# Local attention scores: two heads per matmul, with block-diagonal queries

## The chip, the cores and the metric

The kernel runs on one core of one Trainium2 chip. The metric is the device time of one execution in microseconds (us); lower is better.

Engine names as the profile has them: PE is TensorE, DVE is VectorE, ACT is ScalarE, POOL is GpSimd.

## The reference

Two attention branches over one input x of 2048 positions and width 1024 (32 heads of 32), mixed by a gate. Branch A is linear attention. Branch B, which the change touches, lets each position attend to 8 positions: itself and every second one before it.

```python
def _B_ref(x, wqkv, wo):            # cut: shapes, head transposes
    W, dil = 8, 2
    off = jnp.arange(W) * dil
    idx = pos[:, None] - off[None, :]
    mask = idx >= 0
    ...
    logits = jnp.einsum("bhsd,bhswd->bhsw", q, kg) * scale
    logits = jnp.where(mask[None, None, :, :], logits, -1e9)
    attn = _softmax(logits, axis=-1)
    o = jnp.einsum("bhsw,bhswd->bhsd", attn, vg)
    return ... @ wo

g = _sigmoid((x * gate_w).sum(-1, keepdims=True))
return g * _A_ref(x, A_wqkv, A_wo) + (1 - g) * _B_ref(x, B_wqkv, B_wo)
```

## The kernel before

The kernel loads x with even and odd positions apart, so that the step of 2 becomes a step of 1. A window of 57 queries then needs 64 keys. A *block pair* (in the code a "fill") is two such windows, h = 0 and 1; there are 18 of them. Each has a block of scores, an exponential, a mask, and later a block of values with the sums of the weights:

```python
def fill(e_, qs, nq, offs):                 # nq is 57, or 56 in the last of each half
    ...                                     # loads of the values
    def s_fn(e):
        for c in range(8):                  # 8 groups of 4 heads; head 4c+j on rows 32j
            for h in range(2):
                for j in range(4):
                    last = e.matmul(SO[j].ap(c * nq, (c + 1) * nq)[64 * h:64 * h + 64, :],
                        kT[32 * j:32 * j + 32, c, <64 keys>], qT[32 * j:32 * j + 32, c, <nq queries>],
                        start=True, stop=True, tile_position=(32 * j, 64 * h))
        return last
    P.op("pe", s_fn, 0.55, mode="r", ..., name="S")          # 64 matmuls of 57 columns
    ...                                     # ACT: exp of the scores; DVE: times the mask
    after(PVLAG, values)                    # three slots later: 64 value matmuls and 8 of sums
```

`P.op` only records an operation. A list scheduler written in Python then fixes, before anything runs, the order of the instructions on each engine, by priorities (the order of recording, mostly) and by a table of estimated durations. `slot` is called after each group of 8 dense matmuls, so "two slots later" means about two such groups later:

```python
def slot(rate):
    slot_n[0] += 1
    while later and later[0][0] <= slot_n[0]:
        later.pop(0)[1]()
    ...                                     # starts the next fill when its turn has come
```

Between the fills run dense groups: projections, and the keys of branch A, whose state is summed by blocks of 32 small matmuls ("kv"). When the last state block is done, these operations follow:

```python
# DVE: kva -> kvb, its transpose kvT, then sixteen small copies, which lay out zsel
for c in range(4):
    for r in range(4):
        P.op("dve", lambda e, ...: e.tensor_copy(zsel[32 * r:..., c:8:4, k:k + 1], kva[32 * c:..., r:8:4, 32:33]), 0.1, ...)

def fold(I, jh):                            # state times output weights; called four times
    four = [main.next() for _ in range(4)]  # four of the eight PSUM banks
    ...                                     # 16 matmuls of 32x32 tiles, 512 columns
    for c in range(4):
        move(ws[1][:, 4 * I + c, ...], four[c].ap, 512, four[c], ...)   # four copies out, ACT or DVE

for n, (u, j) in enumerate(nums):           # the queries of branch A, one dense group each
    numer(u, j)                             # one bank; ACT: exp; DVE: two operations
    ...
    if n in (2, 4, 6, 8):
        fold((n - 2) // 4, (n - 2) // 2 % 2)
```

## Time and profile before

| | old kernel |
|---|---|
| time, median | 492.45 us (three runs, 492.34 to 493.23) |
| span of the profiled run | 490.9 us |
| PE busy | 485.7 us, 99% |
| DVE busy | 274.5 us, 56% |
| ACT busy | 166.9 us, 34% |
| score matmuls | 18 blocks of 64 |

From the profile's page of the old kernel: busy time of each engine with its share of the span and its instructions, then the chain that ended last, by engine.

```profile
PE 485.7 (99%) x5123; PEld 226.5 (46%) x5123; DVE 274.5 (56%) x487; ACT 166.9 (34%) x287; POOL 5.1 (1%) x27
...
PE 95%; SPq 2%; DVE 2%; DMA 1%; issue 0%
```

PE bounds the kernel, so a saving counts only if it shortens PE's row, and a delay only if PE waits for it.

The chain in order of time, old kernel, around two score blocks (start in us, duration in us, engine and line; line 1326 are dense matmuls, 1418 scores, 1437 values, 1444 sums):

```profile
126.56 0.63 PE ps_all L1418 x64
127.20 5.29 PE ps_all L1326 x24
132.48 0.21 PE ps_all L1437 x24
132.69 0.19 PE ps_all L1444 x8
132.88 0.32 PE ps_all L1437 x40
...
138.49 0.63 PE ps_all L1418 x63
```

The row of PE is an unbroken alternation of dense groups and small blocks. (One matmul record of 64 is missing in the last line; some records are, so I count weight loads where a count matters.)

The groups of the small matmuls, old kernel (line, engine, operation, shapes, count, then busy us and mean ns of one):

```profile
L1418 PE MATMUL ps_all<-qT,kT 32*64 32x57 bf16 x1024 | 11.2, 200 | 0.0
L1444 PE MATMUL ps_all<-E,ones 64*32 64x456 bf16 x128 | 6.1, 351 | 0.0
```

A mean of 200 ns per matmul says nothing of the cost, because many overlap: in the records used below, the eight matmuls of a round, one on each array tile, start within 0.023 us. What a block costs has to be read from starts.

The table of stretches, old kernel (window in us, its length, then busy time of PE, PEld, DVE, ACT, POOL):

```profile
126.00:319.00 193.00, 193.00 (x3700) 96.13 (x3699) 118.11 (x200) 100.39 (x150) 0.00 (x0) 1.00 0.19 56
319.00:337.00 18.00, 17.94 (x144) 7.15 (x142) 16.34 (x46) 10.11 (x27) 0.00 (x0) 1.00 0.01 2
```

The scores lie where DVE is busy 61% of the time. The second is the stage of the folds that follows.

The old kernel's chain shows the same stage from 319.01 us on, until the second fold:

```profile
319.01 0.44 DVE kva L1527
...
325.79 0.61 DVE pq L1339
...
326.44 0.44 PE ps_all L1571 x16
```

These 7.4 us are nearly all of the chain's 2% for DVE.

### The profile page before, as it was taken

To read this page: it belongs to the slowest core of one execution; us is meant where nothing else is said; L and a number is where in the kernel's file an instruction comes from. 1 tells how busy PE (TensorE), PEld (TensorE's weight loads), DVE (VectorE), ACT (ScalarE), POOL (GpSimd) and SP (SyncE) were. 2 spreads that over 40 slices of the span, in tenths; PEclk is the share of its full clock that TensorE was granted. 3 is DMA by queue.
4 is the path that set the end of the run, shared out by engine and by line. 5 is a ranking of instruction groups with operands and counts; after the bars stand their busy time and mean duration, and the time that the engine had idled before them with its cause. 6 is when DMAs were issued, how large, how long until landed. Compare 5 with 4: busy or idle time off the path is not lost.

```text
span 490.9 us, 11427 instructions
## 1 busy us (share of the span) xinstructions
PE 485.7 (99%) x5123; PEld 226.5 (46%) x5123; DVE 274.5 (56%) x487; ACT 166.9 (34%) x287; POOL 5.1 (1%) x27
## 2 busy tenths in 40 slices
PE   8999999999999999999999999999999999999997
PEld 3444444444444444555454454444444444444443
DVE  2121336899677777465555645596865735334434
ACT  2111121212443344665655556355423323010000
POOL 3000000000000000000000000000000000000000
PEclk9999999999999999999999999999999999999999
DMA  8999993222003045211000100501673406101212
GB/s 208 216 197 271 356 366 100 86 87 85 13 24 109 24 127 146 65 28 43 24 24 24 36 12 4 171 3 22 172 193 80 115 13 180 44 23 45 85 68 89
DMA packets 51069, 48.82 MB, mean 99 GB/s; under 512 B 20161, under 2 KB 38977, under 8 KB 51010
## 3 DMA queue, kind: packets, MB, share of 16 engines
q1 hardware_dynamic: 50322, 47.40, 34.9%
q8 instruction: 42, 0.69, 0.6%
q10 hardware_dynamic: 688, 0.59, 0.4%
q14 instruction: 17, 0.14, 0.1%
HBM read 34.34 MB, written 9.44 MB: 89 GB/s over the span
## 4 chain that ended last, share of the span: by engine, by line
PE 95%; SPq 2%; DVE 2%; DMA 1%; issue 0%
PE ps_all L1326 77%; PE ps_all L1647 11%; PE ps_all L1418 2%; PE ps_all L1437 2%; SPq L1300 1%; PE ps_all L1519 1%; DMA w<-in_B_wqkv_dram 1%; PE ps_all L1444 1%; DVE zsel L1561 1%; SPq L1305 1%; PE ps_all L1598 0%; DVE pq L1339 0%; PE ps_all L1571 0%; DVE e L1337 0%; DVE w L1357 0%
## 5 line engine op out<-in xcount | busy, mean ns | idle before, releaser
L1326 PE MATMUL ps_all<-w,xT 128*128 128x512 bf16 x960 | 213.8, 379 | 0.7 <-DMA xT<-in_A_x_dram 0.6
L1326 PE MATMUL ps_all<-xT,w 128*128 128x512 bf16 x768 | 170.7, 379 | 0.0
L1326 PEld LDWEIGHTS ps_all<-w,xT 128*128 128x128 bf16 x960 | 91.1, 98 | 109.8 <-DMA xT<-in_A_x_dram 2.0
L1326 PEld LDWEIGHTS ps_all<-xT,w 128*128 128x128 bf16 x768 | 73.8, 98 | 89.0 <-issue 1.8
L1647 PE MATMUL ps_all<-w,qT 128*128 128x512 bf16 (+1 forms) x264 | 55.6, 373 | 0.0
L1647 PEld LDWEIGHTS ps_all<-w,qT 128*128 128x128 bf16 x264 | 25.8, 98 | 29.7
L1337 DVE TENSOR_SCALAR e<-e 128x512 bf16<-128x512 bf16 x64 | 18.3, 290 | 34.3 <-ACT e L1335 17.1
L1357 DVE CAST vst<-ps_all 128x512 bf16<-128x512 f32 x15 | 10.4, 691 | 44.3 <-PE ps_all L1326 44.3
L1424 ACT ACTIVATE E<-ps_all 128x1824 bf16<-128x1824 f32 (+1 forms) x18 | 30.4, 1687 | 10.1 <-PE ps_all L1418 9.4
L1335 ACT ACTIVATE e<-ps_all 128x512 bf16<-128x512 f32 x32 | 19.1, 597 | 42.8 <-PE ps_all L1326 42.8
L1427 DVE TENSOR_TENSOR E<-E,msk 128x1824 bf16<-128x1824 bf16 (+1 forms) x18 | 19.8, 1102 | 22.4 <-ACT E L1424 22.4
L1651 DVE SCALAR_TENSOR_TENSOR o<-ps_all,gm,xT 128x512 bf16<-128x512 f32 (+1 forms) x25 | 18.0, 728 | 23.2 <-PE ps_all L1647 22.2
L1333 ACT ACTIVATE e<-ps_all 128x512 bf16<-128x512 f32 x32 | 19.1, 597 | 26.6 <-PE ps_all L1326 25.8
L1358 ACT ACTIVATE vst<-ps_all 128x512 bf16<-128x512 f32 x17 | 10.1, 597 | 49.7 <-PE ps_all L1326 45.5
L1287 DVE TENSOR_TENSOR mx<-mx,kT 128x1024 bf16<-128x1024 bf16 x32 | 20.8, 688 | 9.3 <-ACT kT L1358 9.2
L1287 DVE TENSOR_TENSOR mx<-mx,qT 128x1024 bf16<-128x1024 bf16 x32 | 20.8, 686 | 6.9 <-ACT qT L1361 6.7
L1456 DVE TENSOR_TENSOR qT<-ps_all,L 128x456 bf16<-128x456 f32 (+1 forms) x36 | 21.0, 627 | 6.2 <-ACT L L1454 5.0
L1339 DVE SCALAR_TENSOR_TENSOR pk<-ps_all,e 128x512 bf16<-128x512 f32 x32 | 21.9, 688 | 0.7
L1453 ACT ACTIVATE L<-ps_all 128x456 f32<-128x456 f32 (+1 forms) x36 | 17.8, 547 | 12.4 <-PE ps_all L1437 12.4
L1358 ACT ACTIVATE kT<-ps_all 128x512 bf16<-128x512 f32 x16 | 9.6, 597 | 34.5 <-PE ps_all L1326 34.5
L1361 ACT ACTIVATE qT<-ps_all 128x512 bf16<-128x512 f32 x16 | 9.6, 597 | 31.5 <-PE ps_all L1326 31.5
L1614 DVE TENSOR_TENSOR xT<-xT,rb 128x512 bf16<-128x512 bf16 x24 | 16.2, 688 | 6.6 <-DMA rb<-rc_hbm 6.4
(72 smaller groups left out, 285.6 us busy)
## 6 DMA issues: line engine op xcount, KB each, us to landing
rb<-rc_hbm SPq DMA_DIRECT2D x32, 256.0 KB, 4.8
w<-in_A_wqkv_dram SPq DMA_DIRECT2D x6, 1024.0 KB, 9.3
v<-vB_hbm SPq DMA_DIRECT2D x36, 128.0 KB, 2.8
vB_hbm<-vst SPq DMA_DIRECT2D x32, 128.0 KB, 5.9
w<-in_B_wqkv_dram SPq DMA_DIRECT2D x4, 1024.0 KB, 9.5
xn<-in_A_x_dram SPq DMA_DIRECT2D x16, 256.0 KB, 2.8
out_dram<-o SPq DMA_DIRECT2D x15, 256.0 KB, 2.0
w<-in_A_wo_dram SPq DMA_DIRECT2D x8, 256.0 KB, 3.9
```

The source lines that it names most:

```text
L1287: P.op("dve", lambda e, m=m, op=op: e.tensor_tensor(m[:, 0:n], m[:, 0:n], src, op), 0.08 + n / 1920.0, reads=[m.all(), reg], writes=[m.all()],
L1326: last = e.matmul(bank.ap(), lhs(dc), rhs(dc), start=(dc == 0), stop=(dc == 7))
L1333: P.op("act", lambda e: e.activation(e_[:, :], bank.ap(), ACT.Exp), act(512), reads=[bank.iv], writes=[e_.all()])
L1335: P.op("act", lambda e: e.activation(e_[:, :], bank.ap(), ACT.Exp, accum_out=qe[:, col:col + 1]), act(512) + 0.1, reads=[bank.iv], writes= ...
L1337: P.op("dve", lambda e: e.tensor_scalar(e_[:, :], e_[:, :], 1.0, 1e-6, op0=ALU.min, op1=ALU.add), 0.25, reads=[e_.all()], writes=[e_.all()])
L1339: P.op("dve", lambda e: e.scalar_tensor_tensor(out=dst, in0=bank.ap(), scalar=0.0, in1=e_[:, :], op0=ALU.max, op1=ALU.add), dps(512), read ...
L1358: fa = lambda e: e.activation(dst, src(), ACT.Copy)
L1424: P.op("act", lambda e: e.activation(E[:, 0:32 * nq].rearrange("p (j q) -> p j q", j=4), ps[:, 4:8, 0:8 * nq], ACT.Exp), act(32 * nq), rea ...
L1427: P.op("dve", lambda e: e.tensor_tensor(ev(), ev(), m[:, :, :].rearrange("p r q -> p (r q)")[:, None, :].to_broadcast([128, 16, 2 * nq]), ...
L1456: P.op("dve", lambda e, L=L, h=h, q0=q0: e.tensor_tensor(qT[:, :, q0:q0 + nq], SO[h].ap(0, n).rearrange("p (c q) -> p c q", c=8), L[:, 0:n ...
L1647: last = e.matmul(bank.ap(0, f1 - f0), qT[:, dc, t * 128:(t + 1) * 128], ws[3][:, dc, f0:f1], start=(dc == 0), stop=(dc == 7))
L1651: P.op("dve", lambda e, bank=bank, o_=o_, t=t, n=n, i0=i0, i1=i1, tgt=tgt, c0=c0: e.scalar_tensor_tensor(out=o_[:, i0 * 128:i1 * 128].rear ...
```

## The change

Instead of one head per matmul (32 rows, 57 columns), two heads share one: the keys of two heads are stationary on 64 rows, and the queries come from a tile in which each head's queries stand in their own column half, with zeros in the other half. 32 matmuls of 114 columns replace 64 of 57. The intent is fewer instructions on PE. The price is a tile of queries, made per block pair by two copies with a scalar of 1 or 0 for each partition, and scores issued two slots later, so that the copies are done by then. The diff, cut to its core:

```diff
+    qd = Ring([SB([128, 8, 2, 114], BF16, "qd%d" % i, at=pq0.lo + 4096 * i) for i in range(2)])
+    par = SB([128, 2], F32, "par")                    # cut: eight memsets of 1.0 and 0.0
@@ fill
+            Q, _ = qd.next()
+            for k in range(2):
+                src = qT[:, :, t0 + qs:t0 + qs + 2 * nq]
+                fd = lambda e, k=k: e.tensor_scalar(Q[:, :, k, 0:2 * nq], src, par[:, k:k + 1], None, op0=ALU.mult)
+                fa = lambda e, k=k: e.activation(Q[:, :, k, 0:2 * nq], src, ACT.Copy, scale=par[:, k:k + 1])
+                P.op("any", {"act": fa, "dve": fd}, ...)     # cut: costs, reads, writes
             def s_fn(e):
                 for c in range(8):
                     for h in range(2):
-                        for j in range(4):
-                            last = e.matmul(SO[j].ap(c * nq, (c + 1) * nq)[64 * h:64 * h + 64, :], kT[32 * j:32 * j + 32, c, ...],
-                                            qT[32 * j:32 * j + 32, c, ...], start=True, stop=True, tile_position=(32 * j, 64 * h))
+                        for r in range(2):
+                            c0 = 2 * (c % 4) * nq
+                            last = e.matmul(SO[2 * r + c // 4].ap(c0, c0 + 2 * nq)[64 * h:64 * h + 64, :], kT[64 * r:64 * r + 64, c, ...],
+                                            Q[64 * r:64 * r + 64, c, :, h * nq:(h + 1) * nq], start=True, stop=True, tile_position=(64 * r, 64 * h))
                 return last
-            P.op("pe", s_fn, 0.55, ...)
+            after(2, lambda: rest(e_, qs, nq, t0, k0, m, vt, Q, s_fn))
+        def rest(...):
+            P.op("pe", s_fn, 0.46, ...)               # then exp, mask and values as before
@@ values: the new place of each head in E
-                                                E[64 * h:64 * h + 64, (8 * j + c) * nq:(8 * j + c + 1) * nq], ...
+                                                E[64 * h:64 * h + 64, place(hd) * nq:(place(hd) + 1) * nq], ...
-                            e.matmul(SO[2 + h]..., ones[64 * h:64 * h + 64, :], E[64 * h:64 * h + 64, 8 * j * nq:8 * (j + 1) * nq],
+                            e.matmul(SO[2 + h]..., ones[64 * h:64 * h + 64, :], E[...].rearrange("p (c k q) -> p c k q", k=2, q=nq)[:, :, j % 2, :],
```

More of the change, by code (lines that the diff above doesn't have):

```diff
@@ L1279, in plan @@
         C("dve", lambda e: e.memset(warm[:, :], 0.0), 0.15, [warm.all()])
+        for j in range(4):
+            for k in range(2):
+                C("dve", lambda e, j=j, k=k: e.memset(par[32 * j:32 * j + 32, k:k + 1], 1.0 if j % 2 == k else 0.0), 0.1, [par.all()])
+                P.ops[-1].prio = 1100
         for m in mx[0:2]:
@@ L1403, in plan, with place @@
         slot_n = [0]
+        def place(hd):
+            c, j = hd // 4, hd % 4
+            return 8 * (2 * (j // 2) + c // 4) + 2 * (c % 4) + j % 2
         def fill(e_, qs, nq, offs):
@@ L1412, in fill @@
                      reads=[hb(t0 + k0[h], t0 + k0[h] + 64, i) for i in range(2)], writes=[vt.all()], chan="v%d_%d" % (vslot, h), lat=0.5)
+            Q, _ = qd.next()
+            for k in range(2):
+                src = qT[:, :, t0 + qs:t0 + qs + 2 * nq]
+                fd = lambda e, k=k: e.tensor_scalar(Q[:, :, k, 0:2 * nq], src, par[:, k:k + 1], None, op0=ALU.mult)
+                fa = lambda e, k=k: e.activation(Q[:, :, k, 0:2 * nq], src, ACT.Copy, scale=par[:, k:k + 1])
+                P.op("any", {"act": fa, "dve": fd}, {"act": act(16 * nq), "dve": 0.15 + 16 * nq / 1920.0}, reads=[qT.part((0, 8), (t0 + qs, t0 + qs + 2 * nq)), par.all()],
+                     writes=[Q.part((0, 8), (k, k + 1), (0, 114))])
             def s_fn(e):
@@ L1416, in s_fn, with rest @@
                     for h in range(2):
-                        for j in range(4):
-                            last = e.matmul(SO[j].ap(c * nq, (c + 1) * nq)[64 * h:64 * h + 64, :], kT[32 * j:32 * j + 32, c, t0 + k0[h]:t0 + k0[h] + 64],
-                                            qT[32 * j:32 * j + 32, c, t0 + qs + h * nq:t0 + qs + (h + 1) * nq], start=True, stop=True, tile_position=(32 * j, 64 * h))
-                return last
-            P.op("pe", s_fn, 0.55, mode="r", reads=[kT.part((0, 8), (t0 + k0[0], t0 + k0[1] + 64)), qT.part((0, 8), (t0 + qs, t0 + qs + 2 * nq))],
-                 writes=[s.iv for s in SO], name="S")
+                        for r in range(2):
+                            c0 = 2 * (c % 4) * nq
+                            last = e.matmul(SO[2 * r + c // 4].ap(c0, c0 + 2 * nq)[64 * h:64 * h + 64, :], kT[64 * r:64 * r + 64, c, t0 + k0[h]:t0 + k0[h] + 64],
+                                            Q[64 * r:64 * r + 64, c, :, h * nq:(h + 1) * nq], start=True, stop=True, tile_position=(64 * r, 64 * h))
+                return last
+            after(2, lambda: rest(e_, qs, nq, t0, k0, m, vt, Q, s_fn))
+        def rest(e_, qs, nq, t0, k0, m, vt, Q, s_fn):
+            P.op("pe", s_fn, 0.46, mode="r", reads=[kT.part((0, 8), (t0 + k0[0], t0 + k0[1] + 64)), Q.all()], writes=[s.iv for s in SO], name="S")
             E, _ = Er.next()
@@ L1437, in part @@
                                 last = e.matmul(SO[h].ap(c * nq, (c + 1) * nq)[32 * j:32 * j + 32, :], vt[64 * h:64 * h + 64, hd * 32:hd * 32 + 32],
-                                                E[64 * h:64 * h + 64, (8 * j + c) * nq:(8 * j + c + 1) * nq], start=True, stop=True, tile_position=(64 * h, 32 * j))
+                                                E[64 * h:64 * h + 64, place(hd) * nq:(place(hd) + 1) * nq], start=True, stop=True, tile_position=(64 * h, 32 * j))
                         return last
@@ L1443, in each @@
                         for h in range(2):
-                            e.matmul(SO[2 + h].ap(0, 8 * nq)[32 * j:32 * j + 32, :], ones[64 * h:64 * h + 64, :], E[64 * h:64 * h + 64, 8 * j * nq:8 * (j + 1) * nq],
+                            e.matmul(SO[2 + h].ap(0, 8 * nq)[32 * j:32 * j + 32, :], ones[64 * h:64 * h + 64, :],
+                                     E[64 * h:64 * h + 64, 16 * (j // 2) * nq:16 * (j // 2 + 1) * nq].rearrange("p (c k q) -> p c k q", k=2, q=nq)[:, :, j % 2, :],
                                      start=True, stop=True, tile_position=(64 * h, 32 * j))
```

## The prediction

> **What bounds it now.** PE. The engine table has PE busy 485.7 of 490.9 us, DVE 56%, ACT 34%. The chain of waits is 95% PE, and in the timeline PE has no real gap from 15 to 488 us. So only PE time counts; from 126 to 319 us, where the changed work lies, the table of stretches has PE at 100%, DVE at 61%, ACT at 52%.
>
> **What is touched.** The local scores: 18 blocks of 64 matmuls (line 1418: 32 rows, 57 columns, eight array tiles). The chain gives each block 0.63 us, 2.3% of the span. From single matmul records I take the whole cost: from the last dense matmul before a block to the first after it, less a dense step of 0.216 us, is 0.728 us; 18 make 13.1 us, the most that could be gained (2.7%). Within a block, about 0.09 us pass before the first score matmul, 32 start in 0.14 us, then comes a pause of 0.1 us, the other 32 start every 8.3 ns, and 0.14 us pass before the next dense start. [...]
>
> **After.** 32 pairs[...] on four 64x64 tiles, 114 columns each (half multiply zeros): eight rounds per tile. By the dense 216 ns for 512 columns, 114 take about 48 ns. The fast half's rounds were about 30 ns apart, so a weight load overlaps the preceding matmul; I assume it still does. Eight rounds of 48 to 50 ns plus the 0.21 us that the denominators' blocks (line 1598: two rounds of 0.213 us, 0.641 us in all) show beyond streaming give 0.60 to 0.62 us against 0.728: 0.11 us x 18 = 2.0 us gained.
>
> **Added.** 36 copies of 128x912; the instruction order puts 33 on DVE, 3 on ACT. The existing bf16 tensor-scalar takes 290 ns for 512 elements[...]: 13 us on DVE, no bottleneck. In the order each copy stands ahead of the mask of a block two earlier, so PE shouldn't wait. Scores move two slots later, at no cost. The sums read E in eight runs instead of one: I expect no cost. Fewer small blocks stand side by side (a pair saves 0.06 to 0.1 us): 0.2 us lost, given back by one joined pair of line 1571's.
>
> **Predicted: 490.5 us** (from 492.45), 80% range 489.0 to 492.4. Faster by over 2%: 0.01; within 2%: 0.97; slower by over 2%: 0.02.
>
> **In the profile.** Right: 576 score matmuls; block cost by the records 0.60 to 0.65 us, in even rounds of about 50 ns without the pause; DVE up by 12 to 16 us with copies of about 0.4 us; PE still gapless; the values' and sums' blocks (0.82 us alone) unchanged. Wrong: [...] PE waiting at a block's start.
>
> **What would make it wrong.** Weight loads of 64 rows that don't overlap within a row group[...]. Slow strided reads in the sums (up to some 2 us). A copy late behind DVE's other work, so that PE waits 0.3 us or more 18 times.

## More of the kernel before

PE's timeline in the fold stage, old kernel (start, duration, then the group):

```profile
318.52 0.38 PE L1519 MATMUL ps_all<-az,pk 128*32 128x33 bf16 x32
318.83 3.63 PE L1326 MATMUL ps_all<-xT,w 128*128 128x512 bf16 x16
322.39 0.43 PE L1571 MATMUL ps_all<-w,kvT 32*32 32x512 bf16 x16
322.76 3.63 PE L1326 MATMUL ps_all<-xT,w 128*128 128x512 bf16 x16
326.44 0.44 PE L1571 MATMUL ps_all<-w,kvT 32*32 32x512 bf16 x16
```

After the last state block (line 1519) come two dense groups, a fold, two dense groups, a fold, and so on.

## The result, and the profile after

| | old kernel | changed kernel |
|---|---|---|
| time, median | 492.57 us (4 runs) | 491.72 us (4 runs, 491.08 to 492.20) |
| ratio, with 95% interval | 1 | 0.998 (0.9962 to 0.9997) |
| span of the profiled run | 490.9 us | 489.3 us |
| DVE busy | 274.5 us | 289.2 us |

A ratio is the mean time of one kernel's fast runs over that of the other's of the same rounds, so it is not quite the ratio of the medians beside it. The medians differ by 0.85 us, where I had expected 1.95. The time lies in the predicted range, but 1.1 us of the forecast gain is missing.

The changed kernel's page: engines, then the chain by engine.

```profile
PE 476.7 (97%) x4482; PEld 224.4 (46%) x4547; DVE 289.2 (59%) x531; ACT 167.5 (34%) x287; POOL 5.1 (1%) x27
...
PE 94%; DVE 2%; issue 1%; DMA 1%; SPq 0%
```

The matmuls are 576 fewer, as they should be (4547 weight loads against 5123; 65 matmul records are missing, which is also why PE looks less busy).

The groups that answer to the scores and the sums, and the copies, changed kernel:

```profile
L1438 PE MATMUL ps_all<-qd,kT 64*64 64x114 bf16 x512 | 9.6, 212 | 0.0
...
L1466 PE MATMUL ps_all<-E,ones 64*32 64x456 bf16 x128 | 6.4, 360 | 0.0
```

```profile
L1428 DVE TENSOR_SCALAR qd<-qT,par 128x912 bf16<-128x912 bf16 x29 | 12.4, 453 | 7.6 <-PE ps_all L1438 7.6
```

A copy takes 0.45 us, 33 are on DVE (29 of this shape and 4 for the shorter windows), and DVE is up by 14.7 us. DVE idles before copies for PE (the tile's last readers); PE never idled at a score block for a copy.

The chain in order of time around one score block and the values that follow, changed kernel:

```profile
129.00 0.53 PE ps_all L1438 x32
129.53 0.16 issue
129.69 5.13 PE ps_all L1332 x23
134.82 0.21 PE ps_all L1459 x24
135.02 0.20 PE ps_all L1466 x8
135.22 0.32 PE ps_all L1459 x39
```

The "issue" pieces of 0.16 us are missing records of a dense matmul (23 stand where there are 24), not idleness. So the chain's 0.53 against 0.63 us is about the gain per block.

Single matmul records of one block show how it comes about. Times are in us from the last dense start before the block to the first start of each round (eight matmuls a round in the old kernel, four in the changed one, one on each array tile):

```
old      0.309 0.362 0.394 0.427 | 0.546 0.613 0.680 0.746 | next dense 0.944
changed  0.309 0.387 0.438 0.489   0.540 0.590 0.641 0.693 | next dense but one 1.069
```

The old block runs four rounds (53 ns from the first to the second, then about 33), pauses (0.119 us from the fourth round to the fifth), and then goes on with one matmul every 8.3 ns. The changed block has no pause, and its rounds are 51 ns apart after a first one of 78 ns. In both traces 32 pairs of weight load and matmul come without a pause, and only the old block has more; what makes it pause no run shows, and that a block of 32 would not was my assumption before this trace.

**The cost of a block**, here and below: from a dense start before it to the third dense start after it, less 0.2158 us for each dense matmul between, with matmuls counted by their weight loads. (The prediction ended at the first dense start, which gave 0.728 us; the step after that one is once 10 ns longer, so the same block now reads 0.739.) Added up over the trace, in us:

| | old kernel | changed kernel |
|---|---|---|
| one score block of 57 | 0.739 | 0.638 |
| one value block of 57, alone | 0.833 | 0.836 |
| all score, value and state blocks | 33.60 | 31.96 |
| the four folds | 2.01 | 3.54 |
| the four denominator blocks | 2.71 | 2.61 |
| sum | 38.32 | 38.11 |
| from the 128th dense weight load to the last | 452.73 | 452.52 |
| 128th dense weight load starts at | 34.67 | 33.66 |

So the score, value and state blocks gained 1.64 us, and the folds gave 1.53 us of it back. What the profiled runs differ by beyond that (1.0 us of 1.5) lies before the 128th dense matmul, where the first loads arrive.

PE's timeline in the fold stage, changed kernel:

```profile
315.05 0.38 PE L1542 MATMUL ps_all<-az,pk 128*32 128x33 bf16 x32
315.36 1.90 PE L1332 MATMUL ps_all<-xT,w 128*128 128x512 bf16 x7
317.19 0.27 PE L1459 MATMUL ps_all<-E,v 64*32 64x56 bf16 x24
...
318.13 5.13 PE L1332 MATMUL ps_all<-xT,w 128*128 128x512 bf16 x23 [0.16 <-issue]
323.19 0.43 PE L1594 MATMUL ps_all<-w,kvT 32*32 32x512 bf16 x16
325.18 0.44 PE L1594 MATMUL ps_all<-w,kvT 32*32 32x512 bf16 x16 [1.55 <-DVE w L1363]
325.92 3.40 PE L1332 MATMUL ps_all<-xT,w 128*128 128x512 bf16 x15 [0.30 <-DVE e L1343]
```

The last values (line 1459) now come *after* the last state block, at 317.19, and the first two folds stand side by side. Before the second one PE idles 1.55 us, until DVE has copied a bank out (line 1363). DVE's timeline in the same stretch, changed kernel, shows what it did meanwhile:

```profile
317.07 2.73 DVE L1584 CAST zsel<-kva 32x2 bf16<-32x2 f32 x14
...
321.44 1.15 DVE L1479 TENSOR_TENSOR qT<-ps_all,L 128x448 bf16<-128x448 f32 x2
...
323.75 0.69 DVE L1345 SCALAR_TENSOR_TENSOR pq<-ps_all,e 128x512 bf16<-128x512 f32 x1
324.36 1.28 DVE L1363 CAST w<-ps_all 128x512 bf16<-128x512 f32 x2
```

The fold of 323.19 is copied out by DVE only from 324.36 on, as DVE is still at the queries of branch A (line 1345). The products of the last values (line 1479) stand ahead of them in this stage; in the old kernel they were done before the last state block. The changed kernel's chain confirms it: it runs through DVE from 315.54 to 325.84 us, and the late products are a piece of it:

```profile
321.53 1.06 DVE qT L1479 x2
...
324.44 1.20 DVE w L1363 x2
```

### The profile page after: what moved, and what is told of

Its sections match the earlier page's. It is cut to its first block, busy times and chain, and to the rows that moved or that the text cites. A ratio compares the mean times of both kernels' runs of the same rounds, so it can differ in the third digit from the quotient of the medians.

```text
span 489.3 us, 10251 instructions
## 1 busy us (share of the span) xinstructions
PE 476.7 (97%) x4482; PEld 224.4 (46%) x4547; DVE 289.2 (59%) x531; ACT 167.5 (34%) x287; POOL 5.1 (1%) x27
## 4 chain that ended last, share of the span: by engine, by line
PE 94%; DVE 2%; issue 1%; DMA 1%; SPq 0%
PE ps_all L1332 77%; PE ps_all L1670 11%; PE ps_all L1438 2%; PE ps_all L1459 2%; PE ps_all L1542 1%; DMA xT<-in_A_x_dram 1%; PE ps_all L1466 1%; DVE zsel L1584 1%; DVE pq L1345 1%; PE ps_all L1621 0%; SPq L1306 0%; DVE w L1363 0%; DVE e L1343 0%; DVE qT L1479 0%; SPq L1311 0%
## 5 line engine op out<-in xcount | busy, mean ns | idle before, releaser
L1332 PE MATMUL ps_all<-w,xT 128*128 128x512 bf16 x923 | 208.6, 379 | 4.2 <-issue 3.0
L1332 PE MATMUL ps_all<-xT,w 128*128 128x512 bf16 x747 | 167.5, 379 | 2.5 <-issue 1.7
```

The lines of the kernel that those rows point to most:

```text
L1332: last = e.matmul(bank.ap(), lhs(dc), rhs(dc), start=(dc == 0), stop=(dc == 7))
```

## The experiments

Theory A, from the traces: the score blocks gain 1.6 us; two folds side by side, at a time when DVE is behind, give it back. Its rivals: the start is really faster and the rest nothing (B); the copies' load on DVE is the cause (C); the later scores cost by themselves (D); two folds side by side stall by their demand for banks alone (E). The record marks every run correct, the half-column one too, although that one's result is wrong, so for it the mark says nothing.

### The changed kernel again

No edit.

> The changed kernel once more, unaltered. In its first trace the score blocks cost 0.637 us each, but PE stood 1.6 us before the second of two joined fold blocks, and all that the trace gained on the old kernel (1.5 us of span) lay before the 128th dense matmul, where nothing was changed. Theory A (a real gain of 1.6 us at the score blocks, taken back by the stall at the folds; the rest is chance at the start): from the 128th dense matmul to the last, this trace shows 452.5 us within 0.1 again, fold blocks sum to 3.5 us again, and the ratio to the old kernel lies between 0.997 and 1.000. Theory B (the start is really faster): the stretch before the 128th dense matmul is again near 33.6 us, 1 us below the old kernel's.

Measured: 491.79 us against 492.65, ratio 0.9991 (0.9977 to 1.0004). Folds 3.54 us; 452.58 us from the 128th dense load to the last, which began at 33.88 us. Theory A holds, and the stall is no accident: it is the same within 0.01 us in two traces. B is not told apart by this run, but by later ones: kernels with this very start (runs 3 and 2 below) began at 35.04 and 34.45 us, and one with the old kernel's start (run 5) at 33.79. The start scatters by more than 1 us in either.

### The folds apart

```diff
-            if n in (2, 4, 6, 8):
-                fold((n - 2) // 4, (n - 2) // 2 % 2)
+            if n in (2, 6, 8, 10):
+                fold(*{2: (0, 0), 6: (0, 1), 8: (1, 0), 10: (1, 1)}[n])
```

> The changed kernel with its second, third and fourth fold issued four numerator groups later, so that no two folds stand side by side; nothing else altered. Theory A (the stall comes from two folds side by side, which need eight PSUM banks while the vector engine is behind): the four fold blocks cost 0.46 us each, 1.9 us together instead of 3.5; 1.6 us faster than the changed kernel, ratio to the old kernel 0.9955 to 0.9975. Rival C (the vector engine is behind by the copies, and PE would wait for it wherever the folds stand): PE idles before some later fold or numerator, and the time stays within 0.4 us of the changed kernel.

Measured: 490.66 us against 492.65, ratio 0.9961 (0.9947 to 0.9975). The folds cost 0.471 us each, 1.88 together. PE's timeline of this run, from the first fold:

```profile
323.98 0.43 PE L1594 MATMUL ps_all<-w,kvT 32*32 32x512 bf16 x16
...
327.91 0.43 PE L1594 MATMUL ps_all<-w,kvT 32*32 32x512 bf16 x16
```

The first fold stands just where it stood, behind the last values and 24 dense matmuls; the stall is gone. The late scores and the copies are all still there. So in this kernel the stall needs the two folds side by side, and C is refuted as its sole cause. (The edit moves three folds by two groups each, from n = 4, 6, 8 to 6, 8, 10, and not by four as the expectation says.) The time of the medians fell by 1.1 us rather than 1.6; 0.41 us came back in the trace as a wait at the third denominator block.

### The scores not later

```diff
-            after(2, lambda: rest(e_, qs, nq, t0, k0, m, vt, Q, s_fn))
+            rest(e_, qs, nq, t0, k0, m, vt, Q, s_fn)
```

> The changed kernel with the scores issued at once after the copies, not two slots later. The order of PE around the folds is then the old kernel's: values before the last state, four separate folds. Theory A: folds cost 2.0 us together, no stall, ratio to the old kernel 0.9955 to 0.9975 (1.2 to 2.2 us faster than it). The reason for the two slots would be that PE waits for the copies: if that were so, score blocks would cost more than 0.64 us in some places; theory A expects none of more than 0.65. Rival C: PE waits somewhere all the same, and the time is that of the changed kernel.

Measured: 490.32 us against 492.65, ratio 0.9958 (0.9944 to 0.9972). The folds cost 2.02 us (one waits 0.14), a score block 0.638 us and none more than 0.640; 450.90 us from the 128th dense load to the last, 1.83 less than in the old kernel's trace. PE's timeline of this run is that of the old kernel again:

```profile
317.15 0.38 PE L1542 MATMUL ps_all<-az,pk 128*32 128x33 bf16 x32
317.47 3.63 PE L1332 MATMUL ps_all<-xT,w 128*128 128x512 bf16 x15
321.02 0.43 PE L1594 MATMUL ps_all<-w,kvT 32*32 32x512 bf16 x16
...
325.08 0.44 PE L1594 MATMUL ps_all<-w,kvT 32*32 32x512 bf16 x16
```

The whole expected gain is there once the two slots are taken away, and PE did not need them: it never waits for a copy.

### The copies alone, in the old kernel

The edit is the diff of the change without its scores, values and delay: `qd`, `par` and the 36 copies, with their results unused.

> The old kernel with the 36 copies and their scalars added, their results unused; scores as before from the queries. Theory A: the copies cost nothing on PE: folds 2.0 us together, score blocks 0.728 us, from the 128th dense matmul to the last 452.7 us within 0.2, ratio to the old kernel 0.999 to 1.001. Rival C (the copies' load on the vector engine is the cause of the lost gain): slower than the old kernel by 1 us or more, with PE idle at the folds.

Measured: 492.89 us against 492.65, ratio 1.001 (0.9996 to 1.0024). Folds 2.02 us and score blocks 0.739 us (but for one of 0.801), as in the old kernel. The stretch missed its mark, though: 454.35 us, because PE waited 0.66 and 1.02 us at the second and third denominator blocks (0.95 us in the timeline, for DVE's line 1345, which stood in DVE's queue behind products waiting for loads of reciprocals). The profiled execution was the slowest of its five (493.83 us); the other four, 492.75 to 493.05, show no loss of that size, though the interval allows up to 1.2 us. The test is also weaker than meant: the scheduler put 15 copies on DVE and 21 on ACT here, against 33 and 3. What it shows is that copies alone leave the folds as they were.

### Two folds side by side, in the old kernel

```diff
-            if n in (2, 4, 6, 8):
+            if n in (4, 6, 8):
+                if n == 4:
+                    fold(0, 0)
                 fold((n - 2) // 4, (n - 2) // 2 % 2)
```

> The old kernel, with its first fold issued two numerator groups later, so that the first two folds stand side by side; scores, copies and delay as in the old kernel. Theory A (two folds side by side are what stalls PE): the second fold waits for the vector engine to empty a bank; the fold blocks cost 2.8 to 3.7 us together instead of 2.0, and the kernel is 0.8 to 1.7 us slower than the old one, ratio 1.0015 to 1.0035. Rival C (the stall needs the copies' load or the late last values): folds stay at 2.0 to 2.2 us and the time at that of the old kernel within 0.4 us.

Measured: 493.46 us against 492.15, ratio 1.0029 (1.0016 to 1.0043), slower by 1.3 us. PE's timeline of this run:

```profile
324.96 0.43 PE L1571 MATMUL ps_all<-w,kvT 32*32 32x512 bf16 x16
326.61 0.44 PE L1571 MATMUL ps_all<-w,kvT 32*32 32x512 bf16 x16 [1.22 <-DVE w L1357]
```

The joined pair costs 2.13 us instead of 0.94 for two, and the fold blocks 3.07 together: A's stall, made in the old kernel, without copies and without late scores. (This trace also has 1.6 us at the third denominator block.)

### The delay alone, in the old kernel

```diff
+            after(2, lambda: rest(e_, qs, nq, t0, k0, m, vt, s_fn))
+
+        def rest(e_, qs, nq, t0, k0, m, vt, s_fn):
             P.op("pe", s_fn, 0.55, mode="r", ...
```

> The old kernel with its 64 score matmuls per block issued two slots later, no copies, no new layout. The order keeps four separate folds here. Theory A: nothing is lost: folds 2.0 us together, from the 128th dense matmul to the last 452.7 us within 0.3, ratio 0.999 to 1.001. Rival D (issuing the scores later costs by itself): 1 us or more slower than the old kernel.

Measured: 493.67 us against 492.15, ratio 1.0026 (1.0013 to 1.0040). Theory A missed: the folds are apart (in the trace), and yet the kernel is 1.5 us slower by the medians. PE's timeline of this run:

```profile
323.76 0.43 PE L1574 MATMUL ps_all<-w,kvT 32*32 32x512 bf16 x16
324.12 1.90 PE L1326 MATMUL ps_all<-xT,w 128*128 128x512 bf16 x8
327.02 1.90 PE L1326 MATMUL ps_all<-xT,w 128*128 128x512 bf16 x8 [0.99 <-DVE w L1357]
```

The second dense group after the fold waits 0.99 us for DVE to empty a bank. (The same trace waits 1.49 us more at the third denominator block; this execution, at 495.29 us, was 1.6 us slower than the median of its five.) So A was too narrow. With the last state block later, two of branch A's query groups come ahead of it instead of one. My reading, which no run isolates, is that they and a fold fill the eight banks while DVE is at its small copies, and that whichever instruction of PE needs a bank next has to wait. A side-by-side pair is one way into this, not the only one. D is right so far as this: the delay costs, through what the scheduler then puts where.

### Half the columns

```diff
-                            last = e.matmul(SO[2 * r + c // 4].ap(c0, c0 + 2 * nq)[...], kT[...],
-                                            Q[64 * r:64 * r + 64, c, :, h * nq:(h + 1) * nq], ...
+                            last = e.matmul(SO[2 * r + c // 4].ap(c0, c0 + nq)[...], kT[...],
+                                            Q[64 * r:64 * r + 64, c, 0, h * nq:(h + 1) * nq], ...
```

(The exponential, the mask and the readers of E are cut to that half as well.)

> The changed kernel with only one of the two column halves multiplied: 32 matmuls of 57 columns per block on the same four tiles; the exponential, the mask and the value sums read that half alone. Its result is wrong on purpose. If a round on a tile is set by streaming its 114 columns (my reckoning), rounds fall from 51 ns to about 30 ns, the block from 0.638 to 0.48 to 0.51 us, and the kernel gains about 2.5 us on the changed one. If rounds are set by the weight loads, the block stays above 0.6 us.

Measured: 489.00 us against 492.15, ratio 0.9944 (0.9929 to 0.9959). Rounds of 32 ns after a first of 54, a block of 0.480 us. A round with 114 columns is 51 ns, and 114 columns of a dense matmul's pace (0.2158 us for 512) are an estimated 48 ns: streaming sets the round with 114 columns, as I had reckoned. (With 57 it no longer does alone: 32 ns against an estimated 24.) The zeros cost 0.158 us a block, 2.8 us over 18.

### The old kernel again

No edit; one look.

> The old kernel once more, for a second trace of its start. If the start differs between executions by chance, the 128th dense matmul may begin anywhere from 33.5 to 35.1 us, as the six traces so far do, while from there to the last dense matmul it takes 452.7 us within 0.2. If the old kernel's start is really slower, it begins at 34.6 us or later again.

Measured: 492.76 us. 452.89 us from the 128th dense load to the last, which began at 34.72 us. By this run alone the old kernel's start would look slower. Over all traces, the three with the old kernel's instructions at the start but changes later (runs 5, 6 and 9) began at 33.79, 34.32 and 34.36 us; those with the changed kernel's start between 33.66 and 35.04. I take the start for chance.

### Joined folds, with the small copies on GpSimd

The fifth run's kernel with one more edit:

```diff
-                P.op("dve", lambda e, c=c, r=r, k=k: e.tensor_copy(zsel[...
+                P.op("pool", lambda e, c=c, r=r, k=k: e.tensor_copy(zsel[...
```

> The old kernel with its first two folds side by side, as in the fifth run (2.13 us for the joined pair, fold blocks 3.07 us), but the sixteen small zsel copies, which hold the vector engine for 2.7 us just before the folds, moved to GpSimd. The order of PE is the same, matmul for matmul. Refined theory A (PE stands at the folds because full PSUM banks wait for a vector engine that is behind, by the zsel copies among others): the joined pair falls to 0.9 to 1.3 us, the fold blocks to 1.9 to 2.3 us, and the kernel gains 0.7 to 1.2 us on the fifth run. Rival E (two folds side by side stall by their demand for eight banks alone, whatever the vector engine has to do): the pair stays above 1.8 us.

Measured: 493.64 us against 492.38, ratio 1.0021 (1.0007 to 1.0034). The pair fell from 2.13 to 1.77 us only, the fold blocks from 3.07 to 2.71, and the gain on the fifth run is about 0.4 us by the two ratios, whose intervals overlap. So refined A missed all its marks. PE, DVE and POOL in this run's timeline:

```profile
319.19 4.09 POOL L1561 CAST zsel<-kva 32x2 bf16<-32x2 f32 x16 [196.28 <-DVE kva L1527]
...
325.52 0.43 PE L1571 MATMUL ps_all<-w,kvT 32*32 32x512 bf16 x16
326.07 0.69 DVE L1357 CAST w<-ps_all 128x512 bf16<-128x512 f32 x1 [0.43 <-PE ps_all L1571]
...
326.82 0.44 PE L1571 MATMUL ps_all<-w,kvT 32*32 32x512 bf16 x16 [0.86 <-DVE w L1357]
```

DVE is idle when the first fold ends, starts its copy at once, and PE still waits 0.86 us for it. So E is mostly right about a joined pair (its own mark of 1.8 us was missed by 0.03): the second fold waits for a copy of the first one's results, whatever else DVE has to do. By these two runs DVE's small copies account for the other 0.36 us.

### The changed kernel with the small copies on GpSimd

The same edit, made in the changed kernel.

> The changed kernel, late scores and copies kept, with the sixteen zsel copies on GpSimd. The order of PE changes around the folds: they stand apart, the first one right behind the last values. Refined theory A: no PE stall over 0.2 us at the folds, fold blocks below 2.1 us, 1.4 to 1.8 us faster than the changed kernel, ratio to the old kernel 0.9950 to 0.9975. If the late scores themselves cost time, apart from the vector engine's backlog, PE stalls somewhere from 311 to 337 us for 0.5 us or more.

Measured: 490.73 us against 492.38, ratio 0.9963 (0.9950 to 0.9977), so about 1.4 us faster than the changed kernel by the two ratios (0.9991 and 0.9963; 0.8 us by the first comparison's 0.998). The scheduler now put the folds apart, so this run doesn't tell the free DVE from the parted folds. The expectation of no stall over 0.2 us missed: the first fold stands right behind the last values and waits 0.7 us, for ACT's reading of their sums, and 0.5 us went at the second denominator block.

### The best version

The third run's kernel with the same edit, and beside it the third run's kernel unaltered:

> The third run's kernel (scores issued at once after the copies) with the zsel copies on GpSimd. The third run still had one stall of 0.14 us at a fold. Theory A: that goes, and nothing else changes: 0.1 to 0.3 us faster than the third run's kernel, which chance at the start hides; ratio to the old kernel 0.9945 to 0.9970. GpSimd's copies may be slow: if they end after 333 us, the first denominators wait, and the kernel is slower than the third run's.

> The third run's kernel once more, beside the eleventh on the same chip: ratio to the old kernel 0.9945 to 0.9975, from the 128th dense matmul to the last 450.9 us within 0.2.

Measured: 490.35 us (ratio 0.9957, 0.9943 to 0.9971) and 490.26 us (0.9955, 0.9941 to 0.9968), against 492.38. The folds of the first cost 1.88 us without any wait, but 0.46 us came back at the second denominator block; GpSimd buys nothing here. (Its sixteen copies took 4.09 us in run 9's trace, against 2.6 us on DVE in the old kernel's.) The second repeats the third run: 450.90 us from the 128th dense load to the last, as before. The best version is the changed kernel without its two slots: 2.1 us, or 0.45%, faster than the old kernel by the second ratio.

## Why the prediction was right or wrong

- **PE is the bound; only its row counts.** Right. DVE's 14.7 us more cost PE nothing at the score blocks.
- **Score blocks: 0.728 to about 0.61 us, 2.0 us gained.** Right in mechanism, a little large. By the later measure they went from 0.739 to 0.638, 0.101 us each, 1.8 us for 18. Rounds are 51 ns as estimated and set by streaming (half columns: 32 ns); the block missed 0.61 by the first round, which takes 78 ns instead of 51; why, no run shows.
- **Weight loads overlap on the same tile.** Right. A round of 51 ns that streams for an estimated 48 (114 columns at the dense 0.2158 us for 512) leaves no room for an exposed load, and in the changed kernel's trace a load's record lasts 104 ns (median), two rounds; so the loads overlap here. Where they go meanwhile no run shows.
- **Copies of about 0.4 us, 13 us on DVE, PE not waiting for them.** Right in effect; they take 0.45 us. The 0.4 and the 13 us were my estimate, which no trace had shown. In the changed kernel's trace line 1366 scales 512 fp32 elements by a constant in 0.688 us and by a scalar for each partition in 0.748 us (into four runs of 128), while a cast of line 1363 into 16 runs of 32 takes 0.690 us against 0.688 into one run: there the 0.06 us more goes with the scalar for each partition rather than with the runs.
- **Strided reads of the sums at no cost.** Right: a value block went from 0.833 to 0.836 us.
- **Fewer small blocks side by side: 0.2 us lost.** Right: 1.8 us at the scores came out as 1.64 over all score, value and state blocks.
- **"Scores move two slots later, at no cost", and the 0.2 us "given back by one joined pair of line 1571's".** Wrong, and this is the step that failed. The joined pair cost 2.60 us instead of 0.94 for two separate folds: a loss of 1.66 us where I had entered a gain of 0.2. I saw the pair in the instruction order and priced it by what standing side by side saves, not by the eight banks that it needs, four of which DVE and ACT first have to empty; and I rested on DVE's load over the stage of the scores (61%) and not over the next stage (91%), into which the delay pushed work, although the old kernel's chain already ran through DVE there. Folds apart (1.88 us) or scores not delayed (2.02 us) bring the gain back: ratios 0.9961 and 0.9955 to 0.9958, against my forecast of 0.996.

What stays open: PE waits at the second or third denominator block by amounts between 0 and 1.6 us in these traces, for DVE, which stands behind products that wait for loads; I have no run that tells chance from order there. The traces with the longest of these waits (copies alone, joined folds, delay alone) are of executions 0.9 to 1.6 us slower than the median of their kernel, which speaks for chance. The wait blurs the comparison of single traces by that much (copies alone, delay alone, joined folds), though not the folds' own numbers. That the scheduler joined the folds because of the delayed last values is shown in so far as taking the delay away parts them. The delay is not enough by itself: in the old kernel with the delay alone, and in the changed kernel with the small copies on GpSimd, the folds stand apart. Why the scheduler's estimates joined them I did not trace.

## What to carry to other kernels

When a change delays work in a pipelined schedule, look at the stage where its tail lands, not at the one where it starts, and ask whether the engines there have time to spare. When two blocks come to stand side by side, count the buffers that they hold together and who empties them, before counting what standing side by side saves (here 0.07 to 0.11 us for a pair of a value and a state block, against 1.66 us lost at the folds). And take an allowance such as "two slots later" out once as a test: here it guarded against a wait that did not come when it was taken out, and most of the gain came back.
